# A third outer product of the first expert takes a second Winograd level, and one inner sum of the down weights is formed in place

## The chip, the cores and the metric

The kernel runs on one core of a Trainium2 chip. The metric is the device time of one execution in microseconds (us); lower is better. Three runs of the kernel before gave 1654.76, 1654.96 and 1656.51 us, median 1654.96. All data are fp32.

## The reference

A linear attention without softmax (8 batches, 8 heads, 576 tokens, 64 wide), an RMS norm, and then a mixture of four experts over the 4608 tokens. Every expert works on every token, weighted by its probability; the matmuls of the experts are nearly all of the work.

```python
kv = np.einsum('bhsd,bhse->bhde', k, v)
out = np.einsum('bhsd,bhde->bhse', q, kv)
rms = np.sqrt(np.mean(out * out, axis=-1, keepdims=True) + 1e-06)
x = out / rms * g_norm                      # then reshaped to (4608, 512)
p = domain_probs / (domain_probs.sum(-1, keepdims=True) + 1e-09)
for e in range(4):
    h = np.maximum(x @ w1[e], 0.0)          # w1[e]: 512 x 1024  ("up")
    out += p[:, e:e + 1] * (h @ w2[e])      # w2[e]: 1024 x 512  ("down")
```

## The kernel before, in words

**Chunks and steps.** The 4608 tokens are cut into nine chunks of 512 (eight of one batch each, the ninth of what is left of all). A step is one expert on one chunk: s = 0 to 35, nine per expert. While the first expert works on a chunk, attention makes the next chunk. Its token forms are also kept in DRAM, from where the later experts load them.

**Two levels of Winograd.** A product of 2 x 2 blocks needs eight block products in the plain way and seven in Winograd's, at the price of sums of blocks before and of the products after. "up" does this twice (`up`): seven outer products (m in 1, 6, 2, 5, 3, 7, 4), each made of seven inner ones (mm in `ORDER`), with 128 columns of moving data. "down" has three ways. `down` has seven outer products of one level, each for two halves of the tokens, with 256 columns. `down_deep` has two levels: outer products in groups of two or one, each of seven inner products with 128 columns. In the mixed way (`down(..., mixed=True)`, steps 1 to 6 of the first expert) five outer products (1, 6, 5, 7, 3) are of one level, and 4 and 2 go as one group to `down_deep`. Step 0 and step 35 are of one level in all seven; steps 7 to 34 of two levels in all.

**Banks and evacuation.** PSUM has eight banks, in four pairs: "u1", "u2", "db", "ab". A group of `down_deep` uses three banks: the first for inner products 1, 6, 7 and 4, the second for 2, the third for 5 and 3. Inner product 1 is copied by ACT into the second and third bank as a seed or added to by later products; 6 and 7 are copied into "snap" buffers (ACT), and two blocks are added from a bank and a snap (`total`, DVE). The third bank is of "ab" where the group has two outer products and of "db" where it has one; the second is of "db" in the mixed way, otherwise "ab". One-level products of the first expert use "db". Each outer product ends in `merge`: it is multiplied by the probability and written (ACT, where it is the first in its cell) or added (DVE) to an accumulator in SBUF, and then `send` writes rows of the output (SP for the first expert, POOL with a DRAM addition for the next).

**Inner weights.** For each outer product, `inner` (in `weights_2`) forms four sums of quarter blocks of its weights: 5, 7, 6 and 3, 256 columns each. They go to a "w2y" buffer of 1024 columns. There are two such buffers at first; when attention's k, v and q areas come free, five more. For the first expert, products 2 and 4 get their sums early (key 1.0), the others before step 7. `weights_1` has the same for "up", with sum 7 written over the corner of the weights that only it needs.

**Who sets the order.** `Plan` is a list scheduler that runs on the host while the kernel is built. Each operation has a key (its place in the run of steps), a cost per engine, what it reads and writes, and the kind of buffer that it needs. The planner picks for each engine the next ready operation by its due time, worked back from TensorE's. For each step it tries several random shifts of due times and keeps the one with the least idle TensorE. The chosen order is then fixed: each engine runs its own list in order and waits on semaphores. Operations with `either` may go to DVE or POOL. Buffers ("big", "small", "xf", "w2y" and others) are given by the planner; `later` lists areas that are given over to another kind when their first users are through. A `Buf` with kind None is only a mark for dependencies.

**Lines.** Where the profile names a line: L478 is every fp32 matmul of the experts, L501 every sum by `combine`, L1343 and L1351 the evacuation of "up", L1307 the ReLU, L1662 and L1670 the copies and additions of `down_deep`, L1700 its additions of outer products, L1491 and L1499 the two forms of `merge`, L1515 and L1517 the writes of the output, L1167 the keeping of token forms, L507 loads on SP.

Of the kernel before, what the change touches and what calls it, by code (L numbers as in the profile page):

```python
# [13 lines left out]
ALU = mybir.AluOpType  # L14
AX = mybir.AxisListType
ENG = mybir.EngineType
F32 = mybir.dt.float32
# [342 lines left out]
def kernel(  # L360
# [41 lines left out]
    NT = 512  # L402
# [34 lines left out]
    for kind, n in BANKS.items():  # L437
# [4 lines left out]

    KV = 640
    kv_home = pool.tile([P, 3, 2 * NT], F32, tag="kv", name="kv")
    w2y_home = pool.tile([P, 2, 2 * NT], F32, tag="w2y", name="w2y")
    QW = S * D // 32
    small_home = pool.tile([P, 4 * 2 * NT], F32, tag="small", name="small")
    kv_flat = kv_home[:].rearrange("p n x -> p (n x)")
    slots["kv"] = [kv_flat[:, i * KV:(i + 1) * KV] for i in range(4)]
    slots["kvbd"] = [kv_flat[:, 4 * KV + i * P:4 * KV + (i + 1) * P] for i in range(4)]  # L450
    slots["q"] = [small_home[:, i * QW:(i + 1) * QW] for i in range(2)]
    slots["small"] = [small_home[:, 2 * QW + i * NT:2 * QW + (i + 1) * NT] for i in range(3)]
    slots["w2y"] = [w2y_home[:, i, :] for i in range(2)]
    halved = slots["db"]
    slots["raw"] = [[b[:, i * HN:(i + 1) * HN] for b in halved] for i in range(2)]
    slots["db"] = []
    later = [
        (("raw",), "db", halved),
        (("kv", "kvbd"), "w2y", [kv_home[:, i, :] for i in range(3)]),
        (("q",), "w2y", [small_home[:, 2 * i * NT:2 * (i + 1) * NT] for i in range(2)]),  # L460
        (("small", "q"), "big", [small_home[:, 2 * i * NT:2 * (i + 1) * NT] for i in range(2, 4)]),
    ]
    x_left = dram.tile([P, 4, NT], F32, tag="x_left", name="x_left")
    x_kept = {
# [21 lines left out]
    def either(n):  # L486
        return {"DVE": 0.155 + 0.00104 * n, "POOL": 0.15 + 0.00225 * n}
# [17 lines left out]
    def load(key, buf, dst, src, kb, reads=(), also=()):  # L505
        plan.add(
            key, SPC, lambda eng: nc.sync.dma_start(out=dst(), in_=src), reads=reads,  # L507
            parts=[buf] + list(also), kb=kb,
        )
# [39 lines left out]
            key + 0.8 + 0.8, {"DVE": 1.5}, lambda eng: norm(eng, slice(NR, NBLK)),  # L549
            reads=[probs_later], writes=[probs_later], port=True)  # L550

    w1f, w2f, w2q, w1corner = {}, {}, {}, {}

    ORDER = (1, 6, 2, 5, 7, 4, 3)
    MERGED = (1, 6, 5, 7, 4, 3, 2)
# [2 lines left out]
    def two(ap):  # L558
        return ap.rearrange("p (k t) -> p k t", k=2)
# [5 lines left out]
    def w2_src(e, uh, dh):  # L565
        rows = moe_w2[e][uh * HF:(uh + 1) * HF, dh * HN:(dh + 1) * HN]
        return rows.rearrange("(kt p) d -> p kt d", p=P)
# [75 lines left out]
    def weights_2(e, key, step, deep):  # L643

        f = {n: Buf("big", f"w2_{e}_{n}") for n in (1, 12, 2, 3, 5, 6, 7, 4)}
        for i, (n, uh, dh) in enumerate(((1, 0, 0), (2, 1, 0), (12, 0, 1), (3, 1, 1))):
            load(
                key + i * step, f[n],
                lambda n=n: f[n].ap[:].rearrange("p (k d) -> p k d", k=4),
                w2_src(e, uh, dh), 512 if e else 330,  # L650
            )

        def form(k_, o, a, b, op):
            combine(
                k_, either(1024), lambda: f[o].ap[:], lambda: f[a].ap[:], lambda: f[b].ap[:], op,
                [f[a], f[b]], [f[o]],
            )

        for i, o, b, uh, dh, a in (
            (4, 5, 12, 0, 1, 1), (5, 6, 3, 1, 1, 5), (6, 7, 3, 1, 1, 12), (7, 4, 2, 1, 0, 6)  # L660
        ):
            if e:
                subtract_from(
                    key + i * step, f[o], lambda ap: ap[:].rearrange("p (k d) -> p k d", k=4),
                    f[a], w2_src(e, uh, dh), [f[a]], [f[o]],
                )
            else:
                form(key + i * step, o, b, a, ALU.subtract)
        w2f[e] = f

        def inner(products=OUTER, deep=deep):
            for j, m in enumerate(products):
                x, y = f[m], Buf("w2y", f"w2y_{e}_{m}")
                parts = {}
                for n, (dq, uq) in ((1, (0, 0)), (2, (0, 1)), (21, (1, 0)), (4, (1, 1))):
                    parts[n] = (x, lambda x=x, dq=dq, uq=uq: x.ap[:].rearrange(
                        "p (k d) -> p k d", k=4)[:, 2 * uq:2 * uq + 2, dq * P:(dq + 1) * P])
                for n, at in ((5, 0), (6, 1), (3, 2), (7, 3)):
                    parts[n] = (y, lambda y=y, at=at: two(y.ap[:, at * HN:(at + 1) * HN]))
                for o, a, b, op in (  # L680
                    (5, 21, 4, ALU.add), (7, 1, 21, ALU.subtract), (6, 5, 1, ALU.subtract),
                    (3, 2, 6, ALU.subtract),
                ):
                    combine(
                        deep + j / 7, either(HN), parts[o][1], parts[a][1], parts[b][1], op,
                        [parts[a][0], parts[b][0]], [y],
                    )
                w2q.setdefault(e, {})[m] = parts

        return inner  # L690
# [836 lines left out]
    def down(s, e, c, mixed=False):  # L1527

        h = hidden.pop(s)
        base = s + 1.2  # L1530
        merge, send = result(s, e, c, base)
        order = [m for m in MERGED if not (mixed and m in (2, 4))]
        firsts = []
        for t in range(2):
            banks = {}
            for j, m in enumerate(order):
                key = base + (len(order) * t + j + 0.5) / 14
                kind = "ab" if e and t else "db"
                if m == 1:
                    banks[1] = Buf(kind, f"d1_{s}_{t}")  # L1540
                elif m in (2, 5):
                    banks[2] = Buf("u2" if s == E * NCH - 1 else kind, f"d{m}_{s}_{t}")
                ps = banks[1 if m in (1, 6, 7, 4) else 2]

                def product(eng, m=m, t=t, ps=ps):
                    for kt in range(4):
                        halves_of(
                            ps.ap[:, 0:HN], four(h[m])[:, kt // 2, t, kt % 2, :],
                            rhs=w2f[e][m].ap[:, kt * HN:(kt + 1) * HN],
                            start=(m in (1, 2, 5) and kt == 0), stop=(kt == 3),  # L1550
                            skip_group_check=True,
                        )

                op = plan.add(
                    key, pe(4, HN), product, reads=[h[m], w2f[e][m]], writes=[ps],
                    after=(second[-1:] if m in (1, 5) else []) + firsts[t:t + 1],
                )
                op.marks, op.opens = (ps, HN), m == 1
                if m == 1:
                    firsts.append(op)  # L1560
                if m == order[-1]:
                    second.append(op)
                i, half, fresh = {
                    1: (t, 0, True), 2: (t, 0, False), 6: (t, 1, True), 3: (t, 1, False),
                    5: (2 + t, 1, True), 7: (2 + t, 1, False), 4: (2 + t, 0, True),
                }[m]
                merge(key - 0.4, [ps], lambda ps=ps: ps.ap[:, 0:HN], i, half, fresh)
                if mixed and m == 7:
                    merge(key - 0.4, [ps], lambda ps=ps: ps.ap[:, 0:HN], 2 + t, 0, True)
            if mixed:  # L1570
                continue
            send(base + 0.5 * (t + 1), t)
            send(base + 0.5 * (t + 1), 2 + t)
        if mixed:
            down_deep(s, e, c, ((4, 2),), base + 5 / 7, h, merge, send)

    def down_deep(s, e, c, groups=((1, 6), (7, 5), (4, 2), (3,)), base=None, h=None, merge=None, send=None):

# [9 lines left out]
        for i, group in enumerate(groups):  # L1588
# [34 lines left out]
            for j, mm in enumerate(ORDER):  # L1623
# [3 lines left out]
                def product(eng, group=group, mm=mm, ps=ps, forms=forms):  # L1627
# [10 lines left out]

                op = plan.add(
                    key, pe(2 * n, P), product,  # L1640
                    reads=[b for m in group for b in (w2q[e][m][mm][0], forms[m][mm][0])]
                    + ([ps] if mm == 2 else []),
                    **{"parts" if mm == 2 else "writes": [ps]},
                    after=(inner_last[-2:-1] or primed) + (second[-1:] if mixed else []) if mm == 1 else seeds if mm == 5 else (),
# [67 lines left out]
                        True,  # L1712
                    )

            if mixed:
                out_(4, 1, 0)
                out_(2, 0, 0)
                for i in (2, 3, 0, 1):
                    send(key, i)
            elif i == 0:  # L1720
                add(6, 1, 6)
            elif i == 1:
                add(7, 6, 7)
                add(6, 6, 5)
                add(5, 7, 5)
                out_(5, 1, 1)
            elif i == 2:
                add(4, 7, 4)
                out_(4, 1, 0)
                send(key, 2)  # L1730
                send(key, 3)
                add(2, 1, 2)
                out_(2, 0, 0)
            else:
                add(3, 6, 3)
                out_(3, 0, 1)
                send(key, 0)
                send(key, 1)
# [25 lines left out]
        keep(0, f"h{dh}", x_halves(0)[dh], 512, 1.35)  # L1764
    x_views = {}
    inner = {0: weights_2(0, 0.25, 0.04, 8.2)}
    inner[0]((2, 4), 1.0)
    norm_probs(0.10)
    CHUNKS = {e: list(range(NCH)) for e in range(E)}
    CHUNKS[1].insert(4, CHUNKS[1].pop(0))  # L1770
    for e in range(E):
        for i in range(NCH):
# [16 lines left out]
            if s:  # L1789
                up(s, e, x_views.pop(s))  # L1790
            if s == NCH - 2:
                inner[e]((1, 6, 7, 5, 3), 6.8)
            elif i == 0 and e:
                inner[e]()
            if s >= 1:
# [12 lines left out]
            if NCH - 2 <= s < E * NCH - 1:  # L1808
                down_deep(s, e, c)
            else:  # L1810
                down(s, e, c, 1 <= s < NCH - 2)

    def idle(bank):
        for r in range(4):
# [53 lines left out]
```

## Time and profile before

| what | value |
|---|---|
| median of three runs | 1654.96 us |
| the profiled execution itself | 1657.53 us |
| its span, first to last instruction | 1655.7 us |
| granted TensorE clock, mean | 0.998 |
| first matmul starts, last one ends (from the span's start) | 1.37 us, 1651.30 us |
| HBM read, written | 153.95 MB, 74.19 MB |
| DMA, mean over the span | 140 GB/s |
| share of the chain that ended last: TensorE, DMA | 97%, 2% |

The page divides the span in busy time of each engine, gives the chain of work that ended last (followed back from the last instruction), and groups instructions by line and tile. PE is TensorE's matmul, PEld its weight load, DVE VectorE, ACT ScalarE, POOL GpSimd, SP SyncE. The list of waits gives for each engine what ended its idle times: total us, how many, the longest. The last matmul is followed by one merge of 0.48 us on DVE and the writing of the last rows.

### The profile page before, as it was taken

What the parts mean: (1) busy time and instruction counts of PE and PEld (TensorE: products, weight loads), DVE (VectorE), ACT (ScalarE), POOL (GpSimd) and SP (SyncE); (2) the same over time, 40 slices, a digit from 0 to 9 for tenths busy, and PEclk for the clock granted to TensorE, in tenths of its full rate; (3) what the DMA queues carried; (4) which work ended last, traced back from release to release, by engine and by line L of the source; (5) the groups of instructions that cost most, each with busy time, mean ns of one, the idle gap of its engine ahead of it and who ended that gap; (6) DMA issues with size and microseconds to landing.
All of it is one profiled execution on the core that took longest, in us unless ns stands there. A gap on an engine that the chain in (4) does not pass through costs nothing.

```text
span 1655.7 us, 66633 instructions
## 1 busy us (share of the span) xinstructions
PE 1646.3 (99%) x29010; PEld 1562.4 (94%) x29010; DVE 1243.8 (75%) x2186; ACT 984.6 (59%) x2445; POOL 695.3 (42%) x667
## 2 busy tenths in 40 slices
PE   9999999999999999999999999999999999999998
PEld 5688889888999999999999999999999999999996
DVE  4777768777788878777778777777778787777774
ACT  3465555554566666666566666666666566666662
POOL 3452232233334454453345554344355545444341
PEclk9999999999999999999999999999999999999999
DMA  9975665624466454444558445444577544444442
GB/s 225 224 207 151 197 173 155 162 93 168 148 193 143 118 120 128 122 112 123 156 146 194 114 113 128 108 110 110 141 192 173 121 120 117 117 107 113 117 104 53
DMA packets 202703, 232.46 MB, mean 140 GB/s; under 512 B 92778, under 2 KB 142378, under 8 KB 202410
## 3 DMA queue, kind: packets, MB, share of 16 engines
q1 hardware_dynamic: 178858, 191.41, 38.5%
q0 software_dynamic: 23552, 36.78, 14.5%
q8 instruction: 228, 3.74, 0.9%
q14 instruction: 65, 0.53, 0.1%
HBM read 153.95 MB, written 74.19 MB: 138 GB/s over the span
## 4 chain that ended last, share of the span: by engine, by line
PE 97%; DMA 2%; SPq 0%; DVE 0%; issue 0%; ACT 0%; DVEq 0%
PE u L478 47%; PE db L478 32%; PE ab L478 15%; PE ab L1110 1%; PE ab L1069 1%; PE ab L1042 1%; DMA big<-in_moe_w_dram 1%; DMA big<-in_v_dram 1%; SPq L507 0%; PE u L822 0%; PE db L1078 0%; PE ab L1131 0%; PE ab L881 0%; PE db L861 0%; DVE ss L982 0%
## 5 line engine op out<-in xcount | busy, mean ns | idle before, releaser
L501 DVE TENSOR_TENSOR big<-big,big 128x1024 f32<-128x1024 f32 (+1 forms) x573 | 518.8, 923 | 34.3 <-ACT big L1307 12.4
L478 PE MATMUL u<-xf,big 128*64 128x128 f32 x7072 | 513.7, 273 | 0.0
L478 PEld LDWEIGHTS u<-xf,big 128*64 128x64 f32 x7072 | 412.7, 137 | 4.9 <-issue 0.8
L478 PE MATMUL u<-xf,w1y 128*64 128x128 f32 x5304 | 393.8, 273 | 0.0
L478 PE MATMUL db<-big,big 128*64 128x128 f32 (+1 forms) x4152 | 344.2, 304 | 0.5 <-ACT snap L1662 0.5
L1351 DVE TENSOR_TENSOR big<-u,snap 128x256 f32<-128x256 f32 x460 | 193.1, 421 | 189.4 <-PE u L478 143.1
L478 PEld LDWEIGHTS u<-xf,w1y 128*64 128x64 f32 x5304 | 310.7, 137 | 2.5 <-issue 0.5
L1343 ACT ACTIVATE snap<-u 128x256 f32<-128x256 f32 x490 | 188.1, 384 | 190.7 <-PE u L478 171.8
L478 PEld LDWEIGHTS db<-big,big 128*64 128x64 f32 x4152 | 254.5, 137 | 34.5 <-issue 1.5
L501 POOL TENSOR_TENSOR big<-big,big 128x256 f32<-128x256 f32 (+1 forms) x142 | 193.9, 1367 | 156.4 <-DVE big L501 74.5
L1343 ACT ACTIVATE big<-u 128x256 f32<-128x256 f32 x460 | 175.4, 384 | 66.5 <-PE u L478 42.9
L501 POOL TENSOR_TENSOR big<-big 128x512 f32<-128x512 f32 (+1 forms) x103 | 128.3, 1246 | 186.5 <-DVE big L501 116.2
L1662 ACT ACTIVATE snap<-db 128x256 f32<-128x256 f32 x236 | 84.6, 359 | 136.7 <-PE db L478 122.8
L1307 ACT ACTIVATE big<-big 128x1024 f32<-128x1024 f32 x137 | 144.0, 1051 | 4.5 <-DVE big L501 3.2
L1670 DVE TENSOR_TENSOR big<-ab,snap 128x256 f32<-128x256 f32 x170 | 71.5, 421 | 65.6 <-ACT snap L1662 41.0
L1515 POOL DMA_DIRECT2D out_dram<-big x112 | 97.6, 1122 | 42.6 <-ACT big L1491 34.8
L1343 ACT ACTIVATE u<-u 128x256 f32<-128x256 f32 x245 | 90.8, 372 | 35.0 <-PE u L478 24.3
L478 PE MATMUL db<-small,big 128*64 128x128 f32 (+1 forms) x1344 | 102.1, 274 | 0.0
L478 PE MATMUL ab<-big,big 128*64 128x128 f32 (+1 forms) x1392 | 97.8, 276 | 0.0
L1491 ACT ACTIVATE big<-big,p_all 128x256 f32<-128x256 f32 x190 | 89.7, 500 | 1.4 <-DVE big L1700 0.8
L478 PE MATMUL ab<-kv,big 128*64 128x128 f32 x1280 | 88.4, 273 | 0.0
L478 PE MATMUL db<-kv,big 128*64 128x128 f32 x1264 | 87.7, 273 | 0.0
(202 smaller groups left out, 2293.4 us busy)
## 6 DMA issues: line engine op xcount, KB each, us to landing
xf<-x SPq DMA_DIRECT2D x104, 512.0 KB, 3.7
xf<-x_h SPq DMA_DIRECT2D x85, 256.0 KB, 3.4
xf<-x SPq DMA_DIRECT2D x78, 256.0 KB, 3.7
out_dram<-big POOLq DMA_DIRECT2D x76, 256.0 KB, 6.1
x<-xf SPq DMA_DIRECT2D x36, 512.0 KB, 3.7
big<-in_moe_w_dram SPq DMA_DIRECT2D x31, 512.0 KB, 6.4
x_h<-big SPq DMA_DIRECT2D x18, 512.0 KB, 3.6
big<-in_moe_w_dram POOLq DMA_DIRECT2D x17, 512.0 KB, 6.8
```

The costliest lines, as they stand in the source:

```text
L478: nc.tensor.matmul(out_[cols], lhsT=lhsT[:, cols], rhs=rhs, **kw)
L501: lambda eng: adder(eng).tensor_tensor(out=out_(), in0=a(), in1=b(), op=op),
L1042: nc.tensor.matmul(bank.ap[r * D:(r + 1) * D, o * D:(o + 1) * D], lhsT=ks[r], rhs=vs[r], start=(j == 0), stop=(j == len(sets) - 1), skip_g ...
L1069: nc.tensor.matmul(raw[r].ap[c * D:(c + 1) * D, (o * NR + t) * D:(o * NR + t + 1) * D], lhsT=qt.ap[half, col:col + D], rhs=kv.ap[half, o * ...
L1110: nc.tensor.transpose(turned[o].ap[:, r * P:(r + 1) * P], qt.ap[:, o * NT + r * P:o * NT + (r + 1) * P], ident[:])
L1307: lambda eng: nc.scalar.activation(out=b.ap[:], in_=b.ap[:], func=ACT.Relu),
L1343: lambda eng: nc.scalar.activation(out=where(), in_=ps.ap[:, 0:HN], func=ACT.Copy),
L1351: lambda eng: nc.vector.tensor_tensor(out=block(whole, a, t), in0=src.ap[:, 0:HN], in1=add_.ap[:], op=ALU.add),
L1491: lambda eng: nc.scalar.activation(out=cell(i, half), in_=ap(), func=ACT.Copy, scale=prob()),
L1515: nc.gpsimd.dma_start(out=dst, in_=cell(i)[parts, :], accum_op=ALU.add)
L1662: lambda eng: nc.scalar.activation(out=where(), in_=group_of(ps.ap), func=ACT.Copy),
L1670: lambda eng: nc.vector.tensor_tensor(out=cell(tq, dq), in0=group_of(src.ap), in1=group_of(add_.ap), op=ALU.add,),
```

## The change

The sum 7 of the down weights' inner forms is no longer written to the "w2y" buffer but over the quarter of the weights it is formed from (called 21 before), which is needed for sums 5 and 7 only. A "w2y" buffer then has three parts, 768 columns. The mark `w2corner` orders the in-place sum behind all that still reads that quarter: the outer sums, and one-level products of step 0. The last expert, whose step 35 is of one level, writes its seven sums 7 to two large buffers instead (`apart`).

The room is given out anew: three "w2y" buffers at first in place of two, then four from the k and v area and one from the small area; of the small area three parts become large buffers, where two did and two became "w2y" buffers.

In the mixed way, product 3 of the outer level leaves the one-level order and becomes a group of its own in `down_deep`, after the group (4, 2). Since products 5 and 3 then no longer add up in one bank, product 5 is merged twice, as before into token blocks 2 and 3 and now also into 0 and 1, and product 3 is merged from SBUF. The inner sums for product 3 are formed with those of 2 and 4; all three are added to the plan after step 0's down.

```diff
-    w2y_home = pool.tile([P, 2, 2 * NT], F32, tag="w2y", name="w2y")
+    w2y_home = pool.tile([P, 3, 768], F32, tag="w2y", name="w2y")
     QW = S * D // 32
-    small_home = pool.tile([P, 4 * 2 * NT], F32, tag="small", name="small")
+    small_home = pool.tile([P, 3840], F32, tag="small", name="small")
...
-    slots["w2y"] = [w2y_home[:, i, :] for i in range(2)]
+    slots["w2y"] = [w2y_home[:, i, :] for i in range(3)]
...
-        (("kv", "kvbd"), "w2y", [kv_home[:, i, :] for i in range(3)]),
-        (("q",), "w2y", [small_home[:, 2 * i * NT:2 * (i + 1) * NT] for i in range(2)]),
-        (("small", "q"), "big", [small_home[:, 2 * i * NT:2 * (i + 1) * NT] for i in range(2, 4)]),
+        (("kv", "kvbd"), "w2y", [kv_flat[:, i * 768:(i + 1) * 768] for i in range(4)]),
+        (("q",), "big", [small_home[:, 2 * i * NT:2 * (i + 1) * NT] for i in range(2)]),
+        (("small", "q"), "big", [small_home[:, 4 * NT:6 * NT]]),
+        (("small", "q"), "w2y", [small_home[:, 6 * NT:6 * NT + 768]]),
...
+            apart = [Buf("big", f"w2z_{e}_{i}") for i in range(2)] if e == E - 1 else []
             for j, m in enumerate(products):
-                x, y = f[m], Buf("w2y", f"w2y_{e}_{m}")
+                x, low, y = f[m], corner[m], Buf("w2y", f"w2y_{e}_{m}")
                 parts = {}
-                for n, (dq, uq) in ((1, (0, 0)), (2, (0, 1)), (21, (1, 0)), (4, (1, 1))):
-                    parts[n] = (x, lambda x=x, dq=dq, uq=uq: x.ap[:].rearrange(
-                        "p (k d) -> p k d", k=4)[:, 2 * uq:2 * uq + 2, dq * P:(dq + 1) * P])
-                for n, at in ((5, 0), (6, 1), (3, 2), (7, 3)):
-                    parts[n] = (y, lambda y=y, at=at: two(y.ap[:, at * HN:(at + 1) * HN]))
+                for n, (dq, uq) in ((1, (0, 0)), (2, (0, 1)), (7, (1, 0)), (4, (1, 1))):
+                    parts[n] = (
+                        [x, low] if n == 7 else [x],
+                        lambda x=x, dq=dq, uq=uq: x.ap[:].rearrange(
+                            "p (k d) -> p k d", k=4)[:, 2 * uq:2 * uq + 2, dq * P:(dq + 1) * P])
+                for n, at in ((5, 0), (6, 1), (3, 2)):
+                    parts[n] = ([y], lambda y=y, at=at: two(y.ap[:, at * HN:(at + 1) * HN]))
+                corner_read, corner_at = parts[7]
+                if apart:
+                    z = apart[j // 4]
+                    parts[7] = ([z], lambda z=z, at=j % 4: two(z.ap[:, at * HN:(at + 1) * HN]))
                 for o, a, b, op in (
                     (5, 21, 4, ALU.add), (7, 1, 21, ALU.subtract), (6, 5, 1, ALU.subtract),
                     (3, 2, 6, ALU.subtract),
                 ):
-                    combine(
-                        deep + j / 7, either(HN), parts[o][1], parts[a][1], parts[b][1], op,
-                        [parts[a][0], parts[b][0]], [y],
-                    )
+                    source, reads = (corner_at, corner_read) if a == 21 else parts[a][::-1]
+                    minus, more = (corner_at, corner_read) if b == 21 else parts[b][::-1]
+                    plan_args = (parts[o][1], source, minus, op, reads + more)
+                    if o == 7 and apart:
+                        plan.add(
+                            deep + j / 7, either(HN),
+                            lambda eng, a=plan_args: adder(eng).tensor_tensor(
+                                out=a[0](), in0=a[1](), in1=a[2](), op=ALU.subtract),
+                            reads=plan_args[4], parts=[z], port=True)
+                    else:
+                        combine(
+                            deep + j / 7, either(HN), *plan_args, [low] if o == 7 else [y])
                 w2q.setdefault(e, {})[m] = parts
...
-        order = [m for m in MERGED if not (mixed and m in (2, 4))]
+        order = [m for m in MERGED if not (mixed and m in (2, 4, 3))]
...
-                    key, pe(4, HN), product, reads=[h[m], w2f[e][m]], writes=[ps],
+                    key, pe(4, HN), product, reads=[h[m], w2f[e][m], w2corner[e][m]], writes=[ps],
...
+                if mixed and m == 5:
+                    merge(key - 0.4, [ps], lambda ps=ps: ps.ap[:, 0:HN], t, 1, False)
...
-            down_deep(s, e, c, ((4, 2),), base + 5 / 7, h, merge, send)
+            down_deep(s, e, c, ((4, 2), (3,)), base + 4 / 7, h, merge, send)
...
-            if mixed:
+            if mixed and i == 0:
                 out_(4, 1, 0)
                 out_(2, 0, 0)
-                for i in (2, 3, 0, 1):
-                    send(key, i)
+                send(key, 2)
+                send(key, 3)
+            elif mixed:
+                out_(3, 0, 1)
+                send(key, 0)
+                send(key, 1)
...
-    inner[0]((2, 4), 1.0)
...
-                inner[e]((1, 6, 7, 5, 3), 6.8)
+                inner[e]((1, 6, 7, 5), 6.8)
...
+            if s == 0:
+                inner[0]((2, 4, 3), 1.0)
```

More of the change, by code (lines that the diff above doesn't have):

```diff
@@ L550, in norm_probs @@
             reads=[probs_later], writes=[probs_later], port=True)
-    w1f, w2f, w2q, w1corner = {}, {}, {}, {}
+    w1f, w2f, w2q, w1corner, w2corner = {}, {}, {}, {}, {}
     ORDER = (1, 6, 2, 5, 7, 4, 3)
@@ L645, in weights_2 @@
         f = {n: Buf("big", f"w2_{e}_{n}") for n in (1, 12, 2, 3, 5, 6, 7, 4)}
+        corner = w2corner[e] = {}
         for i, (n, uh, dh) in enumerate(((1, 0, 0), (2, 1, 0), (12, 0, 1), (3, 1, 1))):
+            corner[n] = Buf(None, f"w2c_{e}_{n}")
             load(
@@ L649, in weights_2 @@
                 lambda n=n: f[n].ap[:].rearrange("p (k d) -> p k d", k=4),
-                w2_src(e, uh, dh), 512 if e else 330,
+                w2_src(e, uh, dh), 512 if e else 330, also=[corner[n]],
             )
@@ L655, in form @@
                 k_, either(1024), lambda: f[o].ap[:], lambda: f[a].ap[:], lambda: f[b].ap[:], op,
-                [f[a], f[b]], [f[o]],
+                [f[a], f[b], corner[a], corner[b]], [f[o], corner[o]],
             )
@@ L661, in weights_2 @@
         ):
+            corner[o] = Buf(None, f"w2c_{e}_{o}")
             if e:
@@ L664, in weights_2 @@
                     key + i * step, f[o], lambda ap: ap[:].rearrange("p (k d) -> p k d", k=4),
-                    f[a], w2_src(e, uh, dh), [f[a]], [f[o]],
+                    f[a], w2_src(e, uh, dh), [f[a], corner[a]], [f[o], corner[o]],
                 )
@@ L1640, in down_deep @@
                     key, pe(2 * n, P), product,
-                    reads=[b for m in group for b in (w2q[e][m][mm][0], forms[m][mm][0])]
+                    reads=[b for m in group for b in w2q[e][m][mm][0] + [forms[m][mm][0]]]
                     + ([ps] if mm == 2 else []),
```

## The prediction

> **What bounds the kernel now.** I read the busy line of the page first, then TensorE's waits, then the chain, then the stage that the change touches. Each row: engine, busy us, share, instructions.
>
> ```profile
> PE 1646.3 (99%) x29010; PEld 1562.4 (94%) x29010; DVE 1243.8 (75%) x2186; ACT 984.6 (59%) x2445; POOL 695.3 (42%) x667
> ```
>
> A busy TensorE alone proves little, because matmuls overlap. So the second view, all that TensorE's instructions waited for over the span:
>
> ```profile
> PE u L822 <- DMA big<-in_v_dram: 1.6, 1, 1.6
> PE ab L1816 <- POOL ident masks.py:199: 1.4, 1, 1.4
> PE ab L881 <- DVE big L756: 0.9, 2, 0.8
> PE db L478 <- ACT snap L1662: 0.5, 1, 0.5
> PE ab L1042 <- issue: 0.4, 1, 0.4
> ```
>
> That is 4.8 us, and 3.9 of it (the first three rows) is the opening, before any expert's work. The stream of matmuls sets the time, and the time can only change by the length of that stream or by new waits in it. The chain of waits gives the price of the two kinds of matmul. Columns: start, duration, what. In hardware an fp32 matmul is two instructions, and each half of the output columns is a matmul of its own.
>
> ```profile
> 1616.66 0.87 PE ab L478 x16
> ...
> 1620.59 0.44 PE u L478 x8
> ...
> 1624.52 0.90 PE db L478 x16
> 1625.41 0.02 issue
> 1625.44 0.29 ACT snap L1662
> 1625.72 0.14 issue
> 1625.86 2.97 PE db L478 x32
> 1628.83 1.73 PE u L478 x16
> ```
>
> From 1607.05 to 1613.16 the chain has 112 instructions of 128 columns, back to back: 6.11/112 = 54.6 ns each. From 1628.83 to 1649.55 it has 192 of 256 columns: 20.72/192 = 107.9 ns each. The lines at 1625 are one hand-over without cover: TensorE waits for an ACT copy of its own last product, 0.45 us. Last, the stage of the change beside a later one (window, length, busy PE, PEld, DVE, ACT, POOL, clock, DMA share, GB/s):
>
> ```profile
> 60.00:360.00 300.00, 299.53 (x5092) 257.45 (x5088) 226.89 (x432) 169.75 (x404) 96.26 (x116) 1.00 0.62 171
> 400.00:800.00 400.00, 400.00 (x7242) 396.58 (x7240) 311.41 (x539) 246.31 (x617) 172.12 (x160) 1.00 0.49 130
> ```
>
> The mixed chunks (the first expert's, steps 1 to 6) lie in about 60 to 400 us. There DVE is busy 76%, ACT 57%, POOL 32%. In 400 to 800 us they are at 78, 62 and 43%, and TensorE still has no idle time.
>
> **What the Trainium skill says.** "Perfetto Trace Analysis", section Identifying the Most-Contended Engine: matmul busy share is no measure of headroom, the weight-load share is a better one. The trace agrees: 94% over all and 99 to 100% from 400 to 1600 us, but 86% in the stage of the change, where 256-column matmuls need fewer loads per column. "TensorE: Matmul & The Clock Gate", section Back-to-back issue gap, gives about 81 ns for a sustained load-and-matmul pair at 128 columns. The trace shows 54.6 here, and the measurement decides. "PSUM — Partial Sum Buffer", section PSUM bank collisions, says that two engines may not touch one bank at once in the same quadrant; so the next product into a bank waits for the read of the last. The 0.45 us above is that, or the seed copy, laid bare.
>
> **The change part by part, against the profiled execution (1657.53 us, span 1655.7).**
>
> *TensorE.* Per mixed chunk, the third product of the outer level leaves the one-level path: 2 token halves x 4 blocks of the contraction x 2 column halves x 2 = 32 instructions at 107.9 ns = 3.45 us. It becomes 7 inner products of 2 blocks x 2 halves x 2 = 56 instructions at 54.6 ns = 3.06 us. Difference -0.395 us, over six chunks -2.37 us. The two instruction orders confirm the count: 14588 matmul calls become 14660, that is 12 a chunk, or 144 hardware instructions more. Nothing else on TensorE changes in number.
>
> *Evacuations.* Per chunk: five ACT copies of 128 columns (0.28 us by the L1662 rows of that shape: 278, 277, 262 ns), two DVE additions of 128 columns (0.284, L1670), two more merges on DVE (0.48 by the L1499 rows): product 5 must now be merged into token blocks 0 and 1 apart from product 3, since the two no longer share a bank, and product 3 is merged from SBUF. Also one 512-wide and two 256-wide subtractions for the token forms, on DVE (0.69, 0.42) or POOL (1.28, 0.73). Six chunks: ACT +30 x 0.28 = 8.4 us, DVE 12 x 0.284 + 12 x 0.48 = 9.2, and 9.2 more on DVE or 16.5 on POOL. If all went to DVE, it would rise from 227 to at most 245 us in the 300 shown (82%). I cost this at nothing: TensorE's 300 us of stream cover it, and the later stage bears about that load. If the cover is gone, the price is 0.45 us per bare hand-over, as at 1625.
>
> *In-place sum.* As many sums as before, of the same size (0.42 us on DVE, 0.73 on POOL). The sum 7 now waits until one-level readers of its corner are through. Only the first expert has such readers: products 2, 4, 3 of step 0. In the changed order, priced with the durations above, the last of them ends after 106 us of TensorE work, and the first inner sum is used after 142. Queued behind the sums on POOL and DVE are token forms and the outer level's additions; a chain of four sums of 0.42 to 0.73 us against 36 us of room costs nothing. If the room is gone, DVE and POOL queues are held and the next late thing is the group's fifth product, again a TensorE wait. For experts 1 and 2 no reader is left when the sums run. The last expert keeps its seven sums apart, in two large buffers.
>
> *Buffers.* Large ones: 33 become 34 once the small area is free, less 2 in the last expert. Slots for inner sums: 7 become 8, of 768 instead of 1024 columns. No row of the trace shows a TensorE wait for a buffer; the bound above is the bound of the 400-to-1600 stage, nothing won, and below a stall of some us if one buffer fewer in the last expert holds a load back. I take zero.
>
> *Queues.* The planner draws anew from step 1 on: TensorE's order is the same for its first 378 rows (about 68 us of work), then everything is interleaved differently; no transfer is added or lost (687 on SP, 151 on POOL in both), but some keeps of token forms move ahead of loads of k and v on SP. The DMA share there is 0.62, so I take zero, with 0.3 us for new small waits. I also counted, in both orders, how much other TensorE work lies between two uses of a bank. Closer than two products (0.87 us) are attention's own, 384 and 386 up to 360 us, and next to none later. With just two products between, from 65 to 420 us, there are 32 before and 47 after; but from 420 to 1590 us the kernel before has 287 of these and no TensorE wait listed. The tail is the same order with the same hand-over.
>
> Sum: 1655.7 - 2.37 + 0.3 = 1653.6 span. The profiled run is 2.6 us over the median, so against the median: 1654.96 - 2.37 + 0.3 = **1652.9 us**, 0.12% less. The rest of a measurement's noise is near 0.2% (3.3 us); that is my line between change and no change.
>
> **Rivals.**
>
> *A. Waits saved too (7%).* The waits after the opening (0.5 and 0.4 us) add to 0.9 us; a new order could lose them, and the 0.3 us of new ones might not come. 1654.96 - 2.37 - 0.9 = 1651.7, which noise carries over 0.2% about every other time. Against: the tail's hand-over is in the new order again.
>
> *B. Slower by bare hand-overs (13%).* A group of a single product keeps all three of its banks in "db", which has two, shared with the one-level products, while groups of two use "ab" for the third. Each chunk has about three hand-overs inside the group (seed copy, snap, the next use). At 0.45 us it takes 13 of the 18 to lose 2.37 and 3.3 us more; all 18, with those of the one-level products that come after them, give 1654.96 - 2.37 + 8.1 = 1660.7. For: at 1625 just such a group was caught bare. Against: there nothing was left to interleave, while in the chunks "up" products stand between, as from 400 us on, where a group of one runs in every chunk, its second bank in "ab" though, with no wait listed.
>
> *C. The small matmuls are slower than 54.6 ns (3%).* At the skill's 81 ns the new part costs 56 x 81 = 4.54 us against 3.45, six times +1.08 = +6.5 us: 1661.5. It turns at 3.45/56 = 61.7 ns. Against: 54.6 in every stretch of the chain.
>
> *D. Some waits, nothing measurable (17%).* One to five us of scattered waits, after late forms or late k and v, give 1653.5 to 1657.6.
>
> The forecast itself (60%) has its own range, 1651.9 to 1653.6. Within 0.2% (1651.65 to 1658.27) lie the forecast and D: 0.77. Faster 0.08: half of A, and the forecast's lower edge with noise. Slower 0.15: B and C, less a part of B that stops short. The range of 8 in 10 reaches from 1651.3 (A less some noise) to 1657.5 (most of D).
>
> **What would show it.** TensorE 29154 instructions; its waits still some 5 us, none over 0.5 us between 60 and 400 us; the start of steady deep work some 2.4 us earlier. DVE's and ACT's busy time some 9 to 18 and 8 us higher. Wrong if TensorE shows rows waiting for ACT "snap" or "db" copies, for POOL's in-place sums, or for k and v, in 60 to 400 us, or if the last expert (1240 to 1620 us) shows waits behind weight loads.

## The result, and the profile after

Over 20 runs of each kernel on the same chips the changed kernel takes 1652.91 us (1651.2 to 1656.05), the kernel before 1655.71. The ratio is 0.9983, 95% interval 0.9977 to 0.9989: 2.8 us faster, between 1.8 and 3.8. That is within the 0.2% that the prediction set as its line, and clear of zero.

The profiled execution of the changed kernel took 1653.64 us, its span is 1651.9. Its busy line (engine, busy us, share, instructions):

```profile
PE 1642.9 (99%) x29154; PEld 1563.5 (95%) x29154; DVE 1257.7 (76%) x2211; ACT 988.5 (60%) x2468; POOL 721.5 (44%) x691
```

TensorE has its 144 instructions more and is 3.4 us less busy: more instructions, at about half the spacing of those they replace. All that TensorE waited for over the span:

```profile
PE ab L1061 <- DMA big<-in_v_dram: 1.5, 1, 1.5
PE ab L1842 <- POOL ident masks.py:199: 1.4, 1, 1.4
PE ab L900 <- DVE big L775: 0.9, 2, 0.8
PE db L479 <- ACT snap L1683: 0.4, 1, 0.4
PE u L479 <- DVE big L1370: 0.3, 1, 0.3
```

That is 4.5 us, against 4.8 before, and again the first three rows lie in the first 45 us. (L479 is the matmul line now, L1683 the copies of `down_deep`, L1370 the evacuation of "up".) One wait of 0.3 us is new; it lies in the stage of the change, at 82 us. The windows of that stage and of the next (length, then busy PE, PEld, DVE, ACT, POOL, clock, DMA share, GB/s):

```profile
60.00:360.00 300.00, 299.60 (x5180) 258.39 (x5176) 226.12 (x467) 172.75 (x419) 133.05 (x131) 1.00 0.62 171
400.00:800.00 400.00, 400.00 (x7282) 398.04 (x7280) 320.02 (x549) 247.89 (x623) 180.11 (x164) 1.00 0.49 131
```

TensorE is as full as before. The added elementwise work is there, but not where I had put it: DVE is unchanged, POOL has 37 us more. That is more than the change adds, as sums that DVE made before have gone to POOL too (22 sums of 1024 columns there, where it had 10). The tail by the chain of waits (start, duration, what):

```profile
1616.86 0.44 PE u L479 x8
...
1620.79 0.90 PE db L479 x16
1621.68 0.02 issue
1621.71 0.29 ACT snap L1683
1621.99 0.04 issue
1622.04 2.98 PE db L479 x32
1625.02 1.73 PE u L479 x16
```

The same order with the same bare hand-over (0.35 us here), 3.8 us earlier: the last stretch of one-level products begins at 1625.02 in place of 1628.83. The prices per instruction are those of before.

### The profile page after: what moved, and what is told of

It reads as the page before. It is cut to its first block, busy times and chain, and to the rows that moved or that the text cites. A ratio compares the mean times of both kernels' runs of the same rounds, so it can differ in the third digit from the quotient of the medians.

```text
span 1651.9 us, 66950 instructions
## 1 busy us (share of the span) xinstructions
PE 1642.9 (99%) x29154; PEld 1563.5 (95%) x29154; DVE 1257.7 (76%) x2211; ACT 988.5 (60%) x2468; POOL 721.5 (44%) x691
## 4 chain that ended last, share of the span: by engine, by line
PE 96%; DMA 2%; SPq 1%; DVE 0%; ACT 0%; issue 0%
PE u L479 47%; PE db L479 32%; PE ab L479 15%; SPq L508 1%; DMA big<-in_v_dram 1%; PE ab L1129 1%; PE ab L1088 1%; PE ab L1061 1%; DMA big<-in_q_dram 0%; DMA small<-in_q_dram 0%; DMA x_h<-big 0%; PE db L1097 0%; PE ab L1150 0%; DVE small L1035 0%; ACT big L1138 0%
## 5 line engine op out<-in xcount | busy, mean ns | idle before, releaser
L502 DVE TENSOR_TENSOR big<-big,big 128x256 f32<-128x256 f32 (+1 forms) x529 | 490.5, 945 | 26.5 <-ACT big L1326 7.5
L479 PE MATMUL u<-xf,big 128*64 128x128 f32 x6784 | 495.0, 273 | 0.1
L479 PEld LDWEIGHTS u<-xf,big 128*64 128x64 f32 x6784 | 395.3, 137 | 3.5 <-issue 0.8
L479 PE MATMUL db<-big,big 128*64 128x128 f32 (+1 forms) x5072 | 394.7, 294 | 0.4 <-ACT snap L1683 0.4
L479 PE MATMUL u<-xf,w1y 128*64 128x128 f32 x5304 | 394.7, 273 | 0.0
L502 POOL TENSOR_TENSOR big<-big,big 128x256 f32<-128x256 f32 (+1 forms) x184 | 247.1, 1345 | 227.2 <-DVE big L502 88.2
L1370 DVE TENSOR_TENSOR big<-u,snap 128x256 f32<-128x256 f32 x470 | 197.1, 421 | 188.8 <-PE u L479 137.5
L479 PEld LDWEIGHTS db<-big,big 128*64 128x64 f32 x5072 | 302.8, 137 | 30.5 <-issue 0.7
L479 PEld LDWEIGHTS u<-xf,w1y 128*64 128x64 f32 x5304 | 311.0, 137 | 2.9 <-issue 0.5
L1362 ACT ACTIVATE snap<-u 128x256 f32<-128x256 f32 x490 | 187.1, 382 | 171.6 <-PE u L479 147.0
L1362 ACT ACTIVATE big<-u 128x256 f32<-128x256 f32 x470 | 179.2, 383 | 72.1 <-PE u L479 48.5
L1683 ACT ACTIVATE snap<-db 128x256 f32<-128x256 f32 x248 | 87.7, 354 | 137.0 <-PE db L479 127.9
L502 POOL TENSOR_TENSOR big<-big 128x512 f32<-128x512 f32 (+1 forms) x89 | 109.4, 1231 | 136.1 <-DVE big L502 69.4
L1326 ACT ACTIVATE big<-big 128x1024 f32<-128x1024 f32 x131 | 137.6, 1050 | 3.6 <-DVE big L502 2.7
L1362 ACT ACTIVATE u<-u 128x256 f32<-128x256 f32 x245 | 90.7, 370 | 41.1 <-PE u L479 29.0
L502 DVE TENSOR_TENSOR big<-big 128x512 f32<-128x512 f32 (+1 forms) x139 | 101.3, 732 | 0.1
L479 PE MATMUL ab<-kv,big 128*64 128x128 f32 x1432 | 99.9, 273 | 0.0
L479 PE MATMUL ab<-big,big 128*64 128x128 f32 (+1 forms) x1296 | 90.5, 278 | 0.0
L1721 POOL TENSOR_TENSOR big<-big 128x512 f32<-128x512 f32 x26 | 33.2, 1275 | 121.9 <-DVE big L502 116.6
```

What stands on the lines that cost most here:

```text
L479: nc.tensor.matmul(out_[cols], lhsT=lhsT[:, cols], rhs=rhs, **kw)
L502: lambda eng: adder(eng).tensor_tensor(out=out_(), in0=a(), in1=b(), op=op),
L1326: lambda eng: nc.scalar.activation(out=b.ap[:], in_=b.ap[:], func=ACT.Relu),
L1362: lambda eng: nc.scalar.activation(out=where(), in_=ps.ap[:, 0:HN], func=ACT.Copy),
L1370: lambda eng: nc.vector.tensor_tensor(out=block(whole, a, t), in0=src.ap[:, 0:HN], in1=add_.ap[:], op=ALU.add),
L1683: lambda eng: nc.scalar.activation(out=where(), in_=group_of(ps.ap), func=ACT.Copy),
```

## The experiments

Two theories stand against each other. *Stream*: the time is the length of TensorE's matmul stream; the change shortens it by 2.37 us, all else is hidden. *Order or room*: the planner has drawn a new order and the buffers are new, and a lucky order or one more large buffer gives the gain. Rival B of the prediction, hand-overs laid bare in the "db" banks, is tested as well. Each kernel was timed beside the kernel before; the table is followed by the single experiments. "Stream" is the count of 128-column instructions x 54.58 ns plus that of 256-column ones x 107.9 ns (before: 25384 and 1408; changed: 25720 and 1216). The 107.9 is that of the chain; 54.58 is the mean spacing from start to start between 800 and 1200 us before, where all are of 128 columns. "Rest" is the time from the first matmul's start to the last one's in the profiled execution, less the stream: the opening with its 128 instructions of 512 columns, attention's own matmuls and all waits. The last column leaves the opening out: it counts from eight transposes, TensorE's 855th to 862nd instructions, to the start of the last matmul. Up to there TensorE's order is the same in all twelve kernels. In the profiles of before and after they start at 68.37 and 67.12 us:

```profile
68.37 1.09 PE L1110 MATMUL ab<-ident,small 128*128 128x128 f32 x8
67.12 1.09 PE L1129 MATMUL ab<-ident,small 128*128 128x128 f32 x8
```

| kernel | ratio to before, 95% interval | stream us | rest us | from the transposes us |
|---|---|---|---|---|
| before | 1 | 1537.4 | 112.2 | 1582.5 |
| before, second order | 1.0006 (0.9998 to 1.0014) | 1537.4 | 110.9 | 1583.6 |
| before, third order | 1.0005 (0.9997 to 1.0014) | 1537.4 | 109.8 | 1582.6 |
| changed | 0.9983 (0.9977 to 0.9989) | 1535.0 | 110.7 | 1580.0 |
| changed, second order | 0.9987 (0.9981 to 0.9994) | 1535.0 | 109.8 | 1580.0 |
| changed, third order | 0.9982 (0.9975 to 0.9988) | 1535.0 | 111.2 | 1580.4 |
| in place, product 3 at one level | 1.0009 (1.0001 to 1.0017) | 1537.4 | 111.5 | 1583.9 |
| product 3 at two levels in three chunks | 0.9993 (0.9985 to 1.0001) | 1536.2 | 110.2 | 1581.5 |
| evacuation doubled | 0.9992 (0.9984 to 1.0000) | 1535.0 | 111.9 | 1581.3 |
| evacuation doubled, second order | 0.9986 (0.9979 to 0.9992) | 1535.0 | 111.1 | 1580.0 |
| 48 more matmul instructions | 0.9993 (0.9985 to 1.0001) | 1537.6 | 110.0 | 1581.5 |
| third bank in "ab" | 0.9979 (0.9971 to 0.9987) | 1535.0 | 110.0 | 1579.1 |

**The in-place sum and the buffers alone.**

```diff
-        order = [m for m in MERGED if not (mixed and m in (2, 4, 3))]
+        order = [m for m in MERGED if not (mixed and m in (2, 4))]
...
-            down_deep(s, e, c, ((4, 2), (3,)), base + 4 / 7, h, merge, send)
+            down_deep(s, e, c, ((4, 2),), base + 5 / 7, h, merge, send)
```

(The extra merge of product 5, the sends and the inner sums go back likewise.)

> The changed kernel with its in-place sum and its new buffers, but product 3 of the mixed chunks left at one level as before. If the length of TensorE's stream is all (the prediction), the stream is that of the kernel before, 29010 instructions, and the time is within 0.5 us of it. If the gain came from the room (one large buffer more, one slot for inner sums more) or from the new order, most of 2.8 us is there without the third product.

Measured: 1657.45 against 1656.00 us, 1.4 us slower (0.2 to 2.8). The room alone gains nothing; that rival falls. But the forecast of the stream theory, within 0.5 us of before, is missed too, by about 1 us. The trace shows where: a row of short waits at the start of the second expert, between 460 and 560 us. One of them, by the chain:

```profile
465.36 0.90 PE u L479 x16
...
466.34 0.39 ACT big L1362
466.73 0.94 ACT big L1326
467.67 0.32 ACT snap L1362
467.99 0.04 issue
468.03 0.66 PE u L479 x8
```

ACT copies a bank (L1362) only after a ReLU of 1024 columns (L1326, 0.94 us) that stands before it in its list; TensorE's next product into that bank comes some 0.2 us late. Matmuls overlap, so the list of waits, which wants an idle engine, hardly shows it; the weight loads do:

```profile
468.03 0.42 PEld L479 LDWEIGHTS u<-xf,small 128*64 128x64 f32 x8 [0.29 <-ACT snap L1362]
```

Between 460 and 560 us the weight loads wait 1.5 us in this kernel. In the kernel before they wait for nothing there, but 1.1 us in its second order (the next experiment), which has neither the in-place sum nor the new buffers. Such waits can come with an order alone. Whether the in-place sum or the buffers have a small price of their own is not shown, as they were run alone in one order only. The next experiments ask how much an order is worth.

**Other orders of both kernels.** Nothing but the planner's random numbers is changed, in the kernel before and in the changed one, twice (50000, and 90000):

```diff
-                draw = random.Random(100 * n + step)
+                draw = random.Random(100 * n + step + 50000)
```

> The kernel before with other random numbers in the planner, so another order of the same work. Stream theory with the prediction's 0.3 us for a new order: within 0.5 us of before. If an order is worth as much as the change, it moves by 1 to 3 us either way.

> The changed kernel with those other random numbers. Stream theory: 2.4 us faster than before, within 0.5 us. If the change's 2.8 us were a lucky order, the gain goes to about nothing here.

> The kernel before in a third order of the same work. From the first two orders (0 and +1.0 us, the change's own new order apart) I expect 0 to +1.5 us against before; with these the size of what an order is worth can be told.

> The changed kernel in a third order. Stream theory: 2.4 us under the kernel before in the same kind of order, so -2.8 to -1 us against before. An order theory has no reason for all three orders of the changed kernel to lie under all three of before.

Measured: before 1657.21 and 1656.45 us (their own before: 1656.00, 1655.98), changed 1653.58 and 1653.64. By the ratios, an order moves the kernel before by 1.0 and 0.8 us, each within the interval of nothing. All three orders of the changed kernel are clear of the kernel before, by 2.2 to 3.0 us, and each is below all three of before. A lucky order as the cause of the gain is out. From the three pairs the gain is 2.8, 3.6 and 2.8 us by the medians (2.8, 3.1 and 3.8 by the ratios), somewhat more than the 2.37 us of the stream. The last column shows what lies over it, as far as one execution of each can: from the transposes on, the three pairs differ by 2.6, 3.6 and 2.2 us. The 3.6 us hold the waits of 1.1 us that before has in its second order; the other two are 2.4 us on average, the stream's figure.

**Half of the chunks.** Product 3 at two levels in steps 4 to 6 alone:

```diff
+        third = s >= 4
...
-        order = [m for m in MERGED if not (mixed and m in (2, 4, 3))]
+        order = [m for m in MERGED if not (mixed and m in (2, 4) + (3,) * third)]
```

> The changed kernel with product 3 at two levels in steps 4 to 6 alone, three chunks of six. Stream theory: 3 x 0.395 = 1.2 us faster than before, half of the whole change's 2.37, with 29082 instructions on TensorE. Room or order theory: as much as the whole change, 2.8 us, or something unrelated to the number of chunks.

In this kernel the sums of product 3 are still formed after step 0, so its one-level products in steps 1 to 3 read weights of which a quarter has been overwritten: the kernel leaves out the later forming of these sums, which would keep the output right. The work is that of the text. Measured: 1654.87 against 1656.00 us, 1.1 us faster (0.2 slower to 2.5 faster), with 29082 instructions. Forecast 1.2. Between nothing for no chunk and 2.8 for six, it is the point that a price per chunk demands, though its interval alone would not prove that. From the transposes on it is 1.0 us shorter than before.

**Evacuation work doubled.** In the six chunks, for the new group alone:

```diff
+                twice = 2 if mixed and n == 1 else 1
...
-                    copy(snap[mm], lambda b=snap[mm], g=group_of: g(b.ap), parts=[snap[mm]])
+                    for _ in range(twice):
+                        copy(snap[mm], lambda b=snap[mm], g=group_of: g(b.ap), parts=[snap[mm]])
```

(The block copies, the additions and the token sums are repeated in the same way. The seed copy, which goes into the second bank alone, and the merges are not.)

> The changed kernel with the evacuation work of the new group done twice in each of the six chunks (same values written again): the two snap copies and two block copies on ACT, two additions on DVE, three token sums on DVE or POOL; in all some 6.7 us more on ACT and 12.6 to 20 us more on DVE and POOL. If that work is covered by TensorE's stream, as the prediction costs it: the changed kernel's time, 2.4 to 2.8 us under before, within 0.5 us. If the group's hand-overs between its banks are near their edge (rival B), the doubled copies lay them bare, 18 hand-overs by about 0.3 us longer, up to 5 us: slower than before.

Measured: 1654.86 against 1655.98 us. That is 1.1 us faster than before where 2.4 to 2.8 were forecast, so some 1.5 us had gone somewhere. The two kernels' intervals overlap, but their traces, from the transposes on, are 1.4 us apart. It did not go into the chunks that hold the doubled work: windows 60 to 400 and 460 to 560 us of this kernel,

```profile
60.00:400.00 340.00, 340.00 (x5814) 295.35 (x5812) 262.22 (x534) 200.69 (x496) 159.18 (x159) 1.00 0.59 169
460.00:560.00 100.00, 98.97 (x1798) 97.74 (x1795) 87.96 (x172) 64.08 (x161) 36.89 (x30) 1.00 0.55 145
```

In the first TensorE is busy for all of 340 us. The 1.0 us of idle time is in the second, at the start of the second expert, and the chain there runs through other work:

```profile
507.29 1.77 PE u L479 x32
509.06 0.02 issue
509.08 0.38 ACT snap L1362
509.47 0.95 ACT big L1326
510.42 0.02 issue
510.44 1.23 DVE big L502
511.67 0.06 DVE small L502
511.73 0.19 issue
511.92 0.88 DVE big L502
512.81 0.25 issue
513.06 0.43 DVE big L1370
513.49 0.04 issue
513.53 1.09 PE u L479 x16
```

A ReLU and three sums, two of them of 1024 columns, stand before the DVE addition (L1370) that frees a bank of "up". That looked like the order, not the doubled work; so the same kernel was run in the second order.

> The doubled evacuation work again, in the order of the second set of random numbers. In the first order it ran 1.1 us under before, about 1.5 over the changed kernel, with the waits at 472 to 513 us, after the chunks that hold the doubled work. If those waits belong to that order (stream theory): 2.2 to 2.8 us under before here, and no new waits in 60 to 400 us. If the doubled work itself costs 1.5 us: again about 1 us under before.

Measured: 1653.75 against 1656.08 us, 2.3 us faster, the changed kernel's time in that order; from the transposes on both take 1580.0 us. Its windows:

```profile
60.00:400.00 340.00, 340.00 (x5818) 295.06 (x5814) 262.68 (x542) 201.25 (x499) 155.21 (x151) 1.00 0.60 170
460.00:560.00 100.00, 99.81 (x1822) 99.21 (x1820) 85.44 (x163) 63.30 (x161) 39.98 (x37) 1.00 0.55 144
```

So what was doubled is covered, with as much room again. Rival B falls, as far as the length of these copies goes; that of the seed copy and of the merges was not tried.

**More matmuls.** Inner product 1 of the new group is multiplied twice:

```diff
-                    for o, m in enumerate(group):
+                    for o, m in [x for _ in range(times) for x in enumerate(group)]:
```

> The changed kernel with inner product 1 of the new group multiplied twice in each of the six chunks (the second time starts afresh, so the values are the same): 8 x 6 = 48 instructions of 128 columns more on TensorE. Stream theory: 48 x 54.6 ns = 2.6 us over the changed kernel, which takes back the gain: within 0.5 us of before. If TensorE has slack in those chunks, the changed kernel's time, 2.4 to 2.8 us under before.

Measured: 1655.01 against 1655.98 us, 1.0 us faster (0.2 slower to 2.5 faster). The forecast, 2.6 us over the changed kernel, would be about 0.2 us faster than before, which lies within the interval; it came out nearer 1.8 us over the changed kernel. The changed kernel's own ratio, 0.9983, lies just outside, but the two intervals overlap. TensorE's records have the 48 instructions, and its span of work is 1647.6 us against 1645.7, 1.9 us more: 2.6 of stream, less 0.7 of rest. From the transposes on it is 1.5 us more. The profile lists no wait in 60 to 400 us. What was forecast is therefore shown in kind, and in size only within the ±1 us that an order and an execution carry.

Beside it stands the doubled evacuation, which in this first order measured the same (1654.86 and 1655.01 us), so the times alone do not part the two. The traces do: the doubled evacuation lost its time in waits at 460 to 560 us, and in another order lost none; the added matmuls have no wait there, only a longer stream. They were not run in a second order. So 2.6 us more on TensorE show in the time, while some 23 us more on the other three engines need not. The changed kernel's line for the window shown above:

```profile
60.00:400.00 340.00, 339.60 (x5798) 294.32 (x5796) 255.00 (x522) 194.29 (x472) 150.09 (x152) 1.00 0.61 172
```

**The third bank.**

```diff
-                5: Buf("ab" if n == 2 else "db", f"d3_{s}_{i}"),
+                5: Buf("ab" if n == 2 or mixed else "db", f"d3_{s}_{i}"),
```

> The changed kernel with the third bank of the new group in ab in place of db, so that its three banks no longer share two. If the hand-overs in db cost nothing (the forecast): the changed kernel's time, 2.2 to 2.8 us under before, and an order's worth (about 1 us) either way. If db is tight (rival B, in part): up to 1 to 2 us faster than the changed kernel.

Measured: 1652.57 against 1656.08 us, 3.5 us faster (2.1 to 4.8). That is some 0.7 us better than the changed kernel and within its interval. The trace has 0.9 us less from the transposes on. An order is worth as much, and this kernel has a new one, so it is not shown that "db" is tight; it is at least no worse, and the best time of the study.

## Why the prediction was right

*The time.* 1652.9 us was forecast and 1652.91 measured; against the kernel before on the same chips, 2.8 us in place of the 2.07 that the sum had after its 0.3 us for new waits, which lies within the interval of 1.8 to 3.8. The direction, the size and "within 0.2%" hold. That the last digit agrees is chance: before itself measured 0.75 us higher over 20 runs than in the three shown.

*TensorE's term.* 56 instructions at 54.6 ns for 32 at 107.9: the counts came as forecast, and the prices did not move in the tail's chain. The half dose and the surplus of matmuls agree with it in sign and, within their intervals, in size. Rival C rested on the about 81 ns that the Trainium skill ("TensorE: Matmul & The Clock Gate", section Back-to-back issue gap) gives for a sustained pair of load and matmul at 128 columns. By that rival's estimate the change would have lost 6.5 us. The spacing measured here, 54.6 ns with weight loads of 64 columns, stands against it, and so does the result. One reading of the prediction needs a correction: the weight-load share of 86% in the stage of the change was not 14% of spare room, since 48 more instructions there made TensorE's work 1.5 us longer.

*Evacuation at nothing.* Right, and shown for most of it by doubling: it cost nothing in one order, and in the other the loss lay elsewhere. The split was right for DVE alone. I had 9 to 18 us more on DVE, 8 on ACT and up to 16.5 on POOL; over the whole span they have 13.9, 3.9 and 26.2. ACT has its 30 copies more but seven of attention's fewer, which the planner moved to DVE, and eight sums of 1024 columns and 13 additions of outer products (512) went from DVE to POOL, smaller sums in part the other way. It cost nothing, as no other engine bounds that stage.

*In-place sum and buffers at nothing.* In the changed kernel the in-place sum brought no wait that the profile lists: the only one in 60 to 400 us, 0.3 us, is behind a DVE addition of "up". Alone, with the buffers, it measured 1.4 us slower, not 0; the waits in that kernel's trace lie in the second expert and look like those of an order. The 0.3 us that I set aside for a new order was small: from the transposes on, three orders of before spread over 1.1 us and three of the changed kernel over 0.4. That the change got an order that cost it next to nothing was luck in part.

*The waits.* Forecast: some 5 us, none over 0.5 us between 60 and 400 us. Found: 4.5, and 0.3. The bare hand-over in the tail is a copy into a "snap" buffer in both chains, not the seed copy, which the prediction left open. One sign of the prediction can't be read as it was put, the start of the steady deep work 2.4 us earlier: the last 256-column matmul before the tail starts at 408.9 us in place of 417.8, 8.9 us earlier, but in the new order 96 instructions more (5.2 us) stand behind it.

*Rival A*, waits saved too, hardly came true: the rest is 1.5 us shorter in the changed kernel's profile, but 1.25 us of that is gained before the transposes, where the order is the same, and other orders of the kernel before have as short a rest.

## What to carry to other kernels

Where one engine's stream fills the span, price a change in that stream's instructions alone, by their spacing in the chain (not by the mean duration of overlapping matmuls: 273 ns here, for a spacing of 54.6), and then ask of all other work only whether it is covered. A planner that draws a new order makes every edit a comparison of two orders: learn what an order is worth by drawing it anew with no edit (here up to some 1 us), before a difference of that size is given a cause. Compare two profiles from a place up to which their orders agree, so that what chance does in the opening stays out. And look for short waits in the weight loads too, as the list of idle times misses those below the overlap of matmuls.

## What the runs showed of the hardware

When a load lands is not fixed by the order in which the kernel issues its work. Up to about 38 us the order of every engine and of the loads on SP is the same in all twelve kernels, yet at TensorE's 451st instruction, 36.1 to 38.9 us from the start, the profile of before is 2.1 to 2.8 us behind the other eleven. Part of this is a load of v: before waits 1.6 us for one at 12.8 us (L822), the changed kernel there for none. At 44.1 us the changed kernel loses 1.5 us to a later load of v (L1061), and before nothing. So a profile carries over 2 us of such chance, about what the change brings. Of the 3.8 us between the two spans 1.25 us were there at the transposes, where TensorE's order still is the same, so the spans were no measure of the gain.
